# Attention and a gated feed-forward layer on one core: the order of all operations, the steps of the tiles and the turns at the buffers come from lists in place of ranks

## The chip, the core and the metric

The kernel runs on one core of a Trainium2 chip (trn2). The metric is the device time of one execution in microseconds; the median of several runs counts. One more execution was taken with a profiler, and every row of a trace below comes from that one. The engines are named as in the profile: PE multiplies matrices (PEld is its loading of weights, which runs beside it), DVE, ACT and POOL compute on vectors, and SP issues the DMAs.

## What is computed

The reference, cut to what matters:

```python
k_p = k.reshape(B, H, Sp, pool, D).mean(axis=3)      # B 8, H 8, S 576, D 64, pool 8
v_p = v.reshape(B, H, Sp, pool, D).mean(axis=3)
scores = scale * np.matmul(q, k_p.transpose(0, 1, 3, 2))
attn = np.exp(scores - np.max(scores, axis=-1, keepdims=True))
attn = attn / (np.sum(attn, axis=-1, keepdims=True) + 1e-09)
x = np.matmul(attn, v_p)                             # as 4608 tokens x 512
g = x @ w_gate                                       # 512 x 1536
return (g / (1 + np.exp(-g)) * (x @ w_val)) @ w_out  # 1536 x 512
```

All inputs and outputs are float32. The kernel splits operands into a high and a low 16-bit part and adds three products for each, so that the matmuls run on 16-bit numbers.

## The kernel before

The 4608 tokens are nine tiles of 512. Attention goes in 40 pieces of up to 128 queries (`ask` loads the queries of one, `answer` does the rest: scores on PE at L643, the softmax on ACT and DVE, a transposing DMA at L1357 that writes `pt`, the values on PE at L732 to L735 for the first batch and at L742 to L748 for the others, and the high and low parts of x). For the first batch the low part of x is one DVE instruction at L767; for the other batches a second transposing DMA, L1506, brings x into place.

The hidden layer is 12 chunks of 128 rows. `chunk` loads the two input weights of one chunk (L380), decodes them on ACT and DVE, and sums their sizes (L426 on ACT, then a small matmul on PE, L361); `halves_of` then makes the high and low parts. A step is one chunk of one tile. Tiles 0 and 1 take plain steps (`plain_step`, 24 matmuls at L852 to L854 for a gate and 24 for a value, issued by PE in groups of 3). From tile 2 on nearly all are fast steps (`fast_step`, seven block products by Strassen and Winograd at L957, twelve operations: PE, ACT and DVE take turns). In a fast step the ninth operation is PE's product 7, the tenth an ACT copy (L1026), the eleventh a DVE addition (L1027), and the twelfth PE's product 4, which needs both. Each step ends with a tanh on ACT (L799), two DVE instructions (L802, L807) and a store of the hidden values to DRAM (L982). When all nine tiles are done, the output weights are cut (`sums_of_w_out`, `cut`), and the hidden values come back in blocks (`load_block`) for the last products (L1818, L1833, L1834), which go from about 640 us to the end.

The order is the planner's. Each piece of work is a generator, called a line here as in the source; it yields operations with an engine, a cost in ns and the time from which its operands are there, and it asks for buffers. `Order.run` keeps a clock for each engine by these costs, and always emits the operation that could begin first; among those that could begin within a slack, the one with the smallest rank (the tables `RANK` and `KINDS`, and single numbers such as `KEYS`, `SPLITS` or `CHUNKS` for the early part). Buffers go to whoever asks first by rank, `Order.granted`:

```python
            if kind == "get" and self.pools[name]:
                got = min(self.pools[name], key=lambda g: g[0])
```

The instructions of an engine are emitted in that order and each engine runs its own in that order; semaphores hold an instruction until its operands are there. So a late operand holds all that is behind it on the same engine.

Early on PE also gets matmuls of zeros (`warm`, L1273), which nobody reads. The planner puts one on PE, at 300 ns, whenever it holds PE to be free, until the first step has been taken (the loop of up to 120, which ends by the flag `taken`); there are 35.

Which chunk a tile takes next is decided while planning: `first_steps` takes for tiles 0 and 1 what will have landed soonest, and `tile_steps` chooses for a later tile between plain and fast by what is ready `soon`.

Of the kernel before, what the change touches and what calls it, by code (L numbers as in the profile page):

```python
# [23 lines left out]
LAG = 3  # L24
# [59 lines left out]

class Order:
# [7 lines left out]
    def __init__(self, pools):  # L93
# [5 lines left out]
        self.lines, self.flags, self.count = [], {}, 0  # L99
        self.pools = {name: [(0.0, item) for item in items] for name, items in pools.items()}  # L100
# [50 lines left out]
    def start(self, prio, g, sp=None):  # L151
        self.count += 1
        e = {"prio": (*prio, self.count), "g": g}
# [14 lines left out]

    def granted(self):
        for e in sorted(self.lines, key=self.rank(None)):  # L170
# [7 lines left out]
            if kind == "get" and self.pools[name]:  # L178
                got = min(self.pools[name], key=lambda g: g[0])
# [63 lines left out]
def attention_then_swiglu(  # L243
# [227 lines left out]
    def k_load(b, g, at=None):  # L471
# [3 lines left out]
        else:  # L475
            if g == 0:
# [387 lines left out]
    converting, reserved = set(), {}  # L864

    def fast_weights(c):

        if True:
            t = yield flag(("used", FAST_FROM - 1, c))
            t = max(t, (yield flag(("decoded", 9 + c // 3 if c < 9 else c, 1))))  # L870
            yield flag("room")
            home_f, t0 = yield get("fw")
            while c in reserved:
                t = yield flag(("used", reserved.pop(c), c))
            converting.add(c)
# [157 lines left out]
    def tile_steps(i):  # L1033
# [8 lines left out]
        todo = list(range(NCH))  # L1042

        def soon(name):
            found = order.flags.get(name)
            return found is not None and (found if isinstance(found, float) else found[0]) < order.now + 1500

        for at in range(NCH):
            prio = "step", i + 0.01 * at
            plain = [c for c in todo if c not in converting]  # L1050
            fast = [c for c in todo if c in converting]
            ready = [c for c in fast if soon(("w", c))]
            if not plain or ready and soon(("xc", i)):
                txc, xc = yield flag(("xc", i))
                c = (ready or fast)[0]
                tw = yield flag(("w", c))
                order.start(prio, fast_step(i, at, c, x, xc, un, prio, max(t, txc, tw)))
            else:
                c = plain[0] if i < FAST_FROM else plain[-1]
                reserved[c] = i  # L1060
                order.start(prio, plain_step(i, at, c, x, un, prio, t))
            todo.remove(c)
# [9 lines left out]
    def chunk(c):  # L1072
# [12 lines left out]
        tf = yield flag(("decoded", c - 3, 1)) if c > 2 else flag("start")  # L1085
# [27 lines left out]
    def halves_of(c, i, t):  # L1113
# [5 lines left out]
        order.done(("decoded", c, i), t)  # L1119

# [13 lines left out]
    def decoded():  # L1134
        t = 0
        for c in range(NCH):
            t = max(t, (yield flag(("p2w", c))), (yield flag(("decoded", c, 1))))
# [901 lines left out]
```

## Time and profile before

| | us |
|---|---|
| median of 3 runs | 908.55 |
| the 3 runs | 908.24, 908.55, 914.46 |
| the profiled execution | 906.06 |
| its span, first to last instruction | 904.2 |
| PE busy | 879.0 (97%) |
| DVE busy | 736.9 (81%) |
| ACT busy | 615.9 (68%) |

The span is 1.9 us shorter than the profiled execution's own time; that rest lies before the first and after the last instruction that the profile shows. "Busy" counts the time in which at least one instruction of the engine runs, from the profile's spans. Matmuls overlap, and their ends are modelled.

### The profile page before, as it was taken

Reading aid. Unit: us, or ns where it says so; the run is one execution under the profiler, and the core shown is the slowest. Engines: PE = TensorE matmul, PEld = TensorE weight load, DVE = VectorE, ACT = ScalarE, POOL = GpSimd, SP = SyncE. Lnnn points to the kernel's source line nnn. Section 1 sums busy time; section 2 is a strip of 40 time slices with the busy share of each in tenths; the row PEclk is TensorE's granted clock in tenths of the full one; section 3 lists DMA queues with packets and bytes.
Section 4 is the critical chain, followed back from the end, with each engine's and each line's share of the span. In section 5 each row is a group of like instructions: output and inputs, shape, how many; then the busy total and the mean of one; then the engine's idle time right before and its main releaser. Section 6 shows DMA issues by size and latency. Waiting matters only on the chain. (4 is left out here: it accounts for less than half of the span.)

```text
span 904.2 us, 18233 instructions
## 1 busy us (share of the span) xinstructions
PE 879.0 (97%) x6853; PEld 637.2 (70%) x6872; DVE 736.9 (81%) x1175; ACT 615.9 (68%) x1458; POOL 196.6 (22%) x245
## 2 busy tenths in 40 slices
PE   7889999999999999999999999999999999999998
PEld 4475455457788888888888888888885555555554
DVE  6899898899798888879888867568978887686872
ACT  5899855666767755775766755446657778777783
POOL 2465316757811521110011000022100000000000
PEclk9599999999999999999999999999999999999999
DMA  9948997438476498396475543136472624517101
GB/s 352 344 123 230 230 256 177 104 114 220 99 213 154 115 238 171 110 230 182 125 182 139 128 145 129 71 106 238 159 268 71 207 96 163 210 39 273 60 24 71
DMA packets 139129, 148.41 MB, mean 164 GB/s; under 512 B 85792, under 2 KB 107040, under 8 KB 136736
## 3 DMA queue, kind: packets, MB, share of 16 engines
q1 hardware_dynamic: 139040, 147.24, 56.1%
q8 instruction: 54, 0.88, 0.4%
q14 instruction: 35, 0.29, 0.1%
HBM read 87.29 MB, written 40.89 MB: 142 GB/s over the span
## 5 line engine op out<-in xcount | busy, mean ns | idle before, releaser
L957 PEld LDWEIGHTS <-mixed 128*128 128x128 f16 x1494 | 144.1, 98 | 19.9 <-issue 2.3
L957 PEld LDWEIGHTS <-wgv_h 128*128 128x128 f16 x1328 | 128.2, 98 | 20.9 <-issue 4.0
L1833 PE MATMUL ps<-low,wsh 128*128 128x512 bf16 (+1 forms) x408 | 142.2, 357 | 0.4
L957 PE MATMUL ps<-xc,mixed 128*128 128x256 f16 x996 | 130.0, 273 | 0.2
L957 PE MATMUL ps<-xc,wgv_h 128*128 128x256 f16 x664 | 116.5, 272 | 1.6 <-DVE ps L1027 0.9
L799 ACT ACTIVATE hf<-ps,un 128x512 f32<-128x512 f32 (+1 forms) x111 | 75.2, 678 | 62.1 <-PE ps L957 49.6
L957 PE MATMUL ps<-x,wgv_h 128*128 128x256 f16 x664 | 115.9, 273 | 0.0
L802 DVE SCALAR_TENSOR_TENSOR hf<-hf,ps 128x512 f32<-128x512 f32 (+1 forms) x111 | 74.0, 667 | 29.1 <-ACT hf L799 28.6
L807 DVE SCALAR_TENSOR_TENSOR hf<-ps,un,hf 128x512 f32<-128x512 f32 (+1 forms) x111 | 81.1, 730 | 17.8 <-PE ps L957 15.7
L957 PE MATMUL ps<-x,wgv_l 128*128 128x256 f16 x332 | 90.5, 273 | 0.0
L957 PE MATMUL ps<-xc,wgv_l 128*128 128x256 f16 x332 | 90.4, 272 | 0.0
L853 PE MATMUL ps<-x,wgv_h 128*128 128x512 f16 (+1 forms) x224 | 79.7, 356 | 0.5 <-DVE x L767 0.3
L852 PE MATMUL ps<-x,wgv_h 128*128 128x512 f16 (+1 forms) x224 | 79.9, 357 | 0.1
L854 PE MATMUL ps<-x,wgv_l 128*128 128x512 f16 (+1 forms) x224 | 79.8, 356 | 0.0
L1833 PEld LDWEIGHTS <-wsh 128*128 128x128 bf16 x420 | 41.0, 98 | 45.2 <-issue 7.6
L1834 PE MATMUL ps<-top,wsl 128*128 128x512 bf16 x188 | 71.3, 379 | 0.3
L957 PEld LDWEIGHTS <-wgv_l 128*128 128x128 f16 x664 | 64.9, 98 | 7.6
L957 PE MATMUL ps<-x,mixed 128*128 128x256 f16 x498 | 68.0, 273 | 0.7 <-DVE ps L1022 0.3
L1019 ACT COPY ps<-ps 128x256 f32<-128x256 f32 x83 | 30.6, 369 | 49.9 <-PE ps L957 49.5
L662 ACT ACTIVATE sc<-ps,mx 128x72 f32<-128x72 f32 (+1 forms) x208 | 64.0, 330 | 0.6
L1818 PE MATMUL ps<-more,wsh 128*128 128x512 f32 (+1 forms) x216 | 50.9, 383 | 0.0
L1310 DVE TENSOR_REDUCE box<-in 128x144 f32<-128x1152 f32 x36 | 48.0, 1339 | 3.5 <-DMA in<-kv_parts 3.5
(215 smaller groups left out, 1911.0 us busy)
## 6 DMA issues: line engine op xcount, KB each, us to landing
hd<-hf SPq DMA_DIRECT2D x105, 256.0 KB, 2.3
in<-kv_parts SPq DMA_DIRECT2D x42, 576.0 KB, 5.2
ws<-w_all SPq DMA_DIRECT2D x36, 512.0 KB, 5.1
wgv_h<-hd SPq DMA_DIRECT2D x9, 1536.0 KB, 6.7
wgv_l<-hd SPq DMA_DIRECT2D x9, 1536.0 KB, 7.4
out_t<-ob SPq DMA_DIRECT2D x36, 256.0 KB, 3.6
qt<-q_rows SPq DMA_DIRECT2D x32, 256.0 KB, 4.1
wd<-wf SPq DMA_DIRECT2D x12, 256.0 KB, 2.3
```

The lines of the kernel that those rows point to most:

```text
L662: nc.scalar.activation(sc[:n, h], pss[g][:n, j * SP : (j + 1) * SP], AF.Exp, bias=mx[:n, g, j : j + 1], scale=EXPSCALE, accum_out=sm[:n, h ...
L799: nc.scalar.activation(hf, gate, AF.Tanh, scale=un[:, c, 0:1])
L802: nc.vector.scalar_tensor_tensor(out=hf, in0=hf, scalar=1.0, in1=gate, op0=ALU.add, op1=ALU.mult)
L807: nc.vector.scalar_tensor_tensor(out=out, in0=val, scalar=un[:, c, 2:3], in1=hf, op0=ALU.mult, op1=ALU.mult)
L852: nc.tensor.matmul(o, wh, x["h"][:, j, a:e], start=(j == 0), stop=False)
L853: nc.tensor.matmul(o, wh, x["l"][:, j, a:e], start=False, stop=False)
L854: nc.tensor.matmul(o, wl, x["h"][:, j, a:e], start=False, stop=(j == NJ - 1))
L957: nc.tensor.matmul(o, a, b, start=begin and j + n == 0, stop=j == HJ - 1 and n == 2, skip_group_check=True,)
L1310: nc.vector.tensor_reduce(out=dst, in_=part["in"], axis=AX.X, op=ALU.add)
L1818: nc.tensor.matmul(o, next(w_of(k, c, j)), where[0][c // 2][:, c % 2], start=begin and c == 0, stop=False, skip_group_check=True,)
L1833: nc.tensor.matmul(o, top, where[1][:, c], start=False, stop=False, skip_group_check=True)
L1834: nc.tensor.matmul(o, lo, x_up, start=False, stop=c == HC - 1, skip_group_check=True)
```

## The change

`NAMES` gives a name to each line (the generator's name and its numbers, so `answer.3` is piece 3 and `plain_step.0.10.7.0.512` the step number 10 of tile 0, chunk 7). `TURNS` is one list of 3691 such names in the order in which they get a turn to emit an operation; `listed` takes the first of the next 200 whose line has an operation to emit. `HOLDERS` says for each pool who gets which buffer in turn, `JOBS` which step comes when and whether it is fast. `ZEROS` is 35. Nothing is taken by rank as long as the list has a name that can go. Some flags become stricter: `decoded` with 2 means that both halves of a chunk are there, and product 6 of the last stage waits in the plan for the copy of product 1's sum.

The instructions are the same ones: on each engine the same kinds in the same numbers (12210 rows of matmuls and weight loads on PE, 1177 on DVE, 1228 on ACT, 250 on POOL, 389 on SP), and the steps of all tiles come in the same order of chunks. What differs is which operation stands before which. On PE the order is the old one again from the sixth operation of the last products on (651.9 us in the trace), to the end.

```diff
+AHEAD = 200
+ZEROS = 35
+NAMES = (
+    "keys.0.0 keys.0.1 ask.0 values_load.0.0 warm chunk.0 values_load.0.1 chunk.1 first_fields answer.0 values_in.0.0 ask.1 values_load.0.2 "
...
+TURNS = (
+    "0 1 2 3 4 5 4 5 4 6 7 4 4 7 0 4 4 1 4 1 4 4 8 9 10 9 11 12 9 13 5 5 5 13 9 4 5 14 9 7 5 15 9 7 4 16 15 5 17 18 15 19 7 20 21 5 9 15 9 22 15 "
...
+HOLDERS = {
...
+    "qt": (
+        "2/1 11/1 16/1 20/0 32/0 50/1 69/1 78/1 79/0 90/1 121/0 130/1 143/0 144/1 153/0 157/1 174/0 178/1 192/0 209/1 213/0 230/1 231/0 243/0 244/1 "
...
+JOBS = (
+    (0, 0, 0, 0), (0, 1, 0, 0), (0, 2, 0, 0), (0, 0, 256, 0), (0, 1, 256, 0), (0, 2, 256, 0), (0, 3, 0, 0), (0, 4, 0, 0),
...
+    def holds(self, pool, line, item):
+        listed = self.holders.get(pool)
+        return not listed or listed[0] == (line, label(item))
 
     def granted(self):
...
-            if kind == "get" and self.pools[name]:
-                got = min(self.pools[name], key=lambda g: g[0])
+            free = [g for g in self.pools[name] if self.holds(name, e["name"], g[1])] if kind == "get" else ()
+            if free:
+                got = min(free, key=lambda g: g[0])
+                del self.holders.get(name, [])[:1]
...
+    def listed(self):
+        for n, name in enumerate(self.turns[:AHEAD]):
+            for e in self.lines:
+                if e["name"] == name and e["need"][0] == "op":
+                    self.turns.pop(n)
+                    return max(self.free[e["need"][1].rstrip("+")], self.ready(e)), e
+        return None
+
     def run(self):
         while self.lines:
             if self.granted():
                 continue
-            first = None
-            for engine, free in self.free.items():
+            first = self.listed()
+            for engine, free in {} if first else self.free.items():
...
-        for at in range(NCH):
+        for at, (_, c, _, fast) in enumerate([job for job in JOBS if job[0] == i]):
             prio = "step", i + 0.01 * at
-            plain = [c for c in todo if c not in converting]
-            fast = [c for c in todo if c in converting]
-            ready = [c for c in fast if soon(("w", c))]
-            if not plain or ready and soon(("xc", i)):
+            if fast:
                 txc, xc = yield flag(("xc", i))
-                c = (ready or fast)[0]
...
-        while cuts or rest:
...
+        for i, c, a, _ in [job for job in JOBS if job[0] < 2]:
+            names = needs(i, c, a)
+            for name in names:
+                yield flag(name)
...
-        for _ in range(120):
-            if ("taken", 0, WARM) in order.flags:
-                break
+        for _ in range(ZEROS):
...
-                    if k == 7:
-                        t0 = yield flag(("begun", p, 3, j))
+                    t0 = yield flag(("begun", p, k - 4, j))
```

Three places show what moves. The source's lines are numbered anew by the lists: L1273, L643, L732 and L361 of before are L1588, L983, L1072 and L701 after; L767, L1310, L366 and L680 are L1107, L1625, L706 and L1020; L852 to L854 are L1192 to L1194.

The first place is PE ahead of the first values. `spare` with `qt` are the scores of a piece (here of piece 3), `pt` with `spare` the values (here of piece 1), `wm` the sums of a chunk's weights. Before, eleven zero matmuls stand ahead of these scores (the last two are shown), and the values follow at once:

```order
L1273 LDWEIGHTS zeros
L1273 MATMUL ps<-zeros 128x512
L1273 LDWEIGHTS zeros
L1273 MATMUL ps<-zeros 128x512
L643 MATMUL ps<-spare,qt 128x72 x8
L732 LDWEIGHTS spare
L732 MATMUL ps<-pt,spare 128x128
```

After, nine stand ahead (the last is shown):

```order
L1588 LDWEIGHTS zeros
L1588 MATMUL ps<-zeros 128x512
L983 MATMUL ps<-spare,qt 128x72 x8
L1588 LDWEIGHTS zeros
L1588 MATMUL ps<-zeros 128x512
L701 MATMUL ps<-wm,ones 128x2
L1588 LDWEIGHTS zeros
L1588 MATMUL ps<-zeros 128x512
L1588 LDWEIGHTS zeros
L1588 MATMUL ps<-zeros 128x512
L1072 LDWEIGHTS spare
L1072 MATMUL ps<-pt,spare 128x128
```

The scores of piece 3 move two zero matmuls up, three zero matmuls and the small matmul of chunk 2 now stand between them and the values of piece 1.

The second place is DVE ahead of the low part of x for piece 1 (`x<-ps,rr,x`). Before:

```order
L684 RECIPROCAL ri<-sm 128x8
L366 TENSOR_SCALAR p2w<-ps 128x2
L369 RECIPROCAL sw<-p2w 128x2
L366 TENSOR_SCALAR p2w<-ps 128x2
L369 RECIPROCAL sw<-p2w 128x2
L1310 TENSOR_REDUCE spare<-in 128x144
L767 SCALAR_TENSOR_TENSOR x<-ps,rr,x 128x4x128
```

After:

```order
L706 TENSOR_SCALAR p2w<-ps 128x2
L709 RECIPROCAL sw<-p2w 128x2
L1625 TENSOR_REDUCE spare<-in 128x144
L1020 TENSOR_REDUCE sm<-sc 128x8
L1107 SCALAR_TENSOR_TENSOR x<-ps,rr,x 128x4x128
L732 TENSOR_SCALAR ws<-ws 128x1024
L706 TENSOR_SCALAR p2w<-ps 128x2
L709 RECIPROCAL sw<-p2w 128x2
L1625 TENSOR_REDUCE spare<-in 128x144
```

One reduction of keys and values (the one of `kv_part.1.3`), one pair of scales and one shift of a chunk's weights go behind the low part of x; the row sums of piece 3 (L1020) come ahead of it.

The third place is PE in tile 0's step with chunk 7, at the scores of piece 8. Before:

```order
L852 LDWEIGHTS wgv_h
L852 MATMUL ps<-x,wgv_h 128x512
L853 LDWEIGHTS wgv_h
L853 MATMUL ps<-x,wgv_h 128x512
L854 LDWEIGHTS wgv_l
L854 MATMUL ps<-x,wgv_l 128x512
L643 MATMUL ps<-spare,qt 64x72 x8
L852 LDWEIGHTS wgv_h
L852 MATMUL ps<-x,wgv_h 128x512
```

After:

```order
L1192 LDWEIGHTS wgv_h
L1192 MATMUL ps<-x,wgv_h 128x512
L1193 LDWEIGHTS wgv_h
L1193 MATMUL ps<-x,wgv_h 128x512
L1194 LDWEIGHTS wgv_l
L1194 MATMUL ps<-x,wgv_l 128x512
L983 MATMUL ps<-spare,qt 64x72 x8
L1192 LDWEIGHTS wgv_h
```

The rows read alike, since all groups of a plain step do; what moved is that five groups of three matmuls that stood behind these scores (one of chunk 7, four of chunk 8) now stand ahead of them.

## Rows read from the trace of the kernel before

**Rows 1.** The head of the page and the engines' busy time.

```profile
span 904.2 us, 18233 instructions
PE 879.0 (97%) x6853; PEld 637.2 (70%) x6872; DVE 736.9 (81%) x1175; ACT 615.9 (68%) x1458; POOL 196.6 (22%) x245
```

**Rows 2.** Stretch, length; PE, PEld, DVE, ACT, POOL busy (instructions); granted clock, DMA share, GB/s.

```profile
50.00:100.00 50.00, 45.55 (x364) 29.26 (x365) 47.15 (x84) 46.51 (x146) 29.44 (x41) 1.00 0.74 213
100.00:640.00 540.00, 533.23 (x4947) 424.59 (x4948) 453.02 (x812) 347.87 (x1000) 149.43 (x166) 1.00 0.60 159
650.00:900.00 250.00, 248.84 (x1217) 149.47 (x1234) 187.29 (x189) 179.26 (x211) 0.00 (x0) 1.00 0.39 139
```

**Rows 3.** PE's waits, whole run: total us, times, longest us.

```profile
PE ps L742 <- DMA pt<-half: 3.6, 5, 1.6
PE ps L360 <- DVE mx L523: 3.2, 1, 3.2
PE ps L361 <- ACT wgv_h L426: 2.6, 4, 1.1
PE ps L643 <- ACT sc L662: 1.5, 1, 1.5
PE ps L957 <- DVE ps L1027: 0.9, 4, 0.3
PE ps L732 <- DMA pt<-half: 0.5, 1, 0.5
```

**Rows 4.** PE in order of time: start, length, instruction, idle time before it.

```profile
19.57 1.24 PE L1273 MATMUL ps<-zeros 128*128 128x512 f16 x3
24.05 0.59 PE L360 MATMUL ps<-least,ones 128*128 128x1 f32 x2 [3.25 <-DVE mx L523]
26.78 1.99 PE L643 MATMUL ps<-spare,qt 64*128 64x72 f32 x16 [1.26 <-DMA qt<-q_rows]
28.70 7.01 PE L1273 MATMUL ps<-zeros 128*128 128x512 f16 x11
35.64 1.99 PE L643 MATMUL ps<-spare,qt 64*128 64x72 f32 x16
37.56 0.29 PE L732 MATMUL ps<-pt,spare 128*128 128x128 f16 x1
42.57 0.27 PE L732 MATMUL ps<-pt,spare 128*128 128x128 f16 x1
46.25 0.27 PE L853 MATMUL ps<-x,wgv_h 128*128 128x256 f16 x1 [0.31 <-DVE x L767]
99.88 0.71 PE L643 MATMUL ps<-spare,qt 64*64 64x72 f32 x14 [1.46 <-ACT sc L662]
243.36 0.39 PE L742 MATMUL ps<-box,pt 128*128 128x512 f16 x1 [1.63 <-DMA pt<-half]
```

**Rows 5.** SP's queue in order of time.

```profile
1.66 1.33 SPq L627 DMA_DIRECT2D qt<-q_rows  x2
17.82 0.55 SPq L627 DMA_DIRECT2D qt<-q_rows  x1
```

**Rows 6.** DVE and ACT ahead of the first step, in order of time.

```profile
39.49 0.69 ACT L763 ACTIVATE x<-ps,rr 128x512 f16<-128x512 f32 x1 [1.42 <-PE ps L735]
40.52 1.33 DVE L1310 TENSOR_REDUCE spare<-in 128x144 f32<-128x1152 f32 x1
41.77 0.74 DVE L767 SCALAR_TENSOR_TENSOR x<-ps,rr,x 128x512 f16<-128x512 f32 x1
45.50 0.70 DVE L767 SCALAR_TENSOR_TENSOR x<-ps,rr,x 128x512 f16<-128x512 f32 x1
```

**Rows 7.** Granted clock around PE's first long wait, columns as in rows 2.

```profile
20.00:24.00 4.00, 0.75 (x2) 0.10 (x1) 2.95 (x7) 4.00 (x7) 0.25 (x1) 0.99 1.01 394
36.00:40.00 4.00, 4.00 (x36) 3.87 (x35) 3.66 (x8) 2.58 (x7) 1.87 (x3) 0.50 1.03 410
44.00:48.00 4.00, 3.64 (x42) 2.61 (x40) 3.78 (x8) 3.53 (x4) 1.15 (x1) 0.95 0.98 230
```

More of the change, by code (lines that the diff above doesn't have):

```diff
@@ new lines, with named, label @@
+JOBS = (
[14 rows of a table added]
+)
+def named(g):
+    code, given, name = g.gi_code, g.gi_frame.f_locals, [g.gi_code.co_name]
+    for arg in code.co_varnames[: code.co_argcount]:
+        v = given[arg]
+        if isinstance(v, dict):
+            name += [v[key] for key in ("i", "a", "n") if key in v]
+        elif type(v) in (int, str) and arg not in ("t", "t0", "t1", "ts", "tn", "tv"):
+            name.append(v)
+    return ".".join(str(v).replace(" ", "") for v in name)
+def label(item):
+    return str(item[-1] if isinstance(item, tuple) else getattr(item, "__name__", item))
@@ L99, in __init__ @@
         self.lines, self.flags, self.count = [], {}, 0
+        names = NAMES.split()
+        self.turns = [names[int(n)] for n in TURNS.split()]
+        self.holders = {pool: [(names[int(n.split('/')[0])], n.split('/')[1]) for n in given.split()] for pool, given in HOLDERS.items()}
         self.pools = {name: [(0.0, item) for item in items] for name, items in pools.items()}
@@ L152, in start @@
         self.count += 1
-        e = {"prio": (*prio, self.count), "g": g}
+        e = {"prio": (*prio, self.count), "g": g, "name": named(g)}
         e["sp"] = e["prio"] if sp is None else (prio[0], sp, self.count)
@@ L863, in attention_then_swiglu @@
     order.idle = idle
-    converting, reserved = set(), {}
     def fast_weights(c):
         if True:
-            t = yield flag(("used", FAST_FROM - 1, c))
-            t = max(t, (yield flag(("decoded", 9 + c // 3 if c < 9 else c, 1))))
+            t = 0
+            for i in sorted({i for i, n, _, fast in JOBS if n == c and not fast}):
+                t = max(t, (yield flag(("used", i, c))))
+            t = max(t, (yield flag(("decoded", 9 + c // 3 if c < 9 else c, 2))))
             yield flag("room")
             home_f, t0 = yield get("fw")
-            while c in reserved:
-                t = yield flag(("used", reserved.pop(c), c))
-            converting.add(c)
             f = home_f("fw")
@@ L1119, in halves_of @@
         order.done(("decoded", c, i), t)
+        t = max(t, split_at.setdefault(c, t))
+        if (c, "one") in split_at:
+            order.done(("decoded", c, 2), t)
+        split_at[c, "one"] = t
     def factors(c, t):
@@ L1162, in first_steps @@
     def first_steps():
-        cuts = [(c, a) for a in (0, HT) for c in range(LAG)] + [(c, 0) for c in range(LAG, NCH)]
-        rest = list(range(NCH))
         taken = [0, 0]
```

108 lines of the change are left out of this document (79 added, 29 removed), and 222 rows, old and new, of tables (HOLDERS, JOBS, NAMES, TURNS).

## The prediction

> **What bounds the kernel now.** I read the engines' shares first, then the busy time by stretch, then PE's waits, and last the order of time at the places where these waits lie. PE is busy for 879.0 of 904.2 us [rows 1], so all that another order can give back is the 25.2 us in which PE stands still, and time in which it works on what nobody needs. By stretch [rows 2]: from 100 to 640 us, where the steps of the tiles run, PE stands for 540 - 533.2 = 6.8 us; from 50 to 100 us for 4.4 us; from 650 to 900 us for 1.2 us. The other 25.2 - 6.8 - 4.4 - 1.2 = 12.8 us lie ahead of 50 us and behind 900 us. Ahead of 50 us PE isn't the bound: the first real step begins at 46.25 us, when the low part of x is there [rows 4], and PE fills its time with zeros. From 50 to 100 us all three large engines are nearly full (DVE 47.2, ACT 46.5, PE 45.6 of 50 us) [rows 2]: there a wait that goes may come back as another.
>
> **The change, part by part.** No instruction comes or goes, on any engine, and the tiles take their chunks in the old order. So there is no new work to price; the sum is made of waits, against the profiled execution's span of 904.2 us, and the result is taken off the median, 908.55 us (the profiled execution itself took 906.06).
>
> *The way to the first step.* The chain before is: values of piece 1 on PE at 37.56, high part of x on ACT at 39.49, low part on DVE at 41.77, values of piece 0 at 42.57 (there is one bank for them, so they wait for the low part), the low part of piece 0 at 45.50, the first step at 46.25 [rows 4, 6]. Three things move on it. First, before, SP loads the queries of piece 3 third of all, at 1.66 us with those of piece 0, and those of piece 2 only at 17.82, behind much other traffic [rows 5]; they arrive late enough for PE to wait 1.26 us at 26.78 [rows 4]. After, the queries of piece 3 and three of the loads that stood ahead of piece 2's come behind these. The scores of piece 2 should then follow the small matmul at 24.05 nearly at once, 1 to 2 us sooner. Second, between these scores and the values of piece 1 stand 11 zeros and the scores of piece 3 before (7.01 and 1.99 us); after it is 12 zeros and one small matmul more, at 7.01 / 11 = 0.64 us a zero. So the values of piece 1 come 0.3 to 1.3 us sooner; I take 0.7. Third, on DVE the low part of piece 1 loses the reduction ahead of it (1.33 us) and gets the row sums of piece 3 in exchange, which are ready earlier. The high part was done at 39.49 + 0.69 = 40.18, the low part began 1.59 us later; I take 1.3 of that. Together 2.0 us at the first step. Since DVE is full from 50 us on, I count 1.5; bounds 0 (DVE gives nothing on) and 3 us.
>
> *Long waits of PE behind the first step.* Each has its producer and its cover in the two orders, so I compare how far PE's instruction moved with how far its producer moved. The scores of piece 8 waited 1.46 us at 99.88 for an exponential; five groups of three matmuls of plain steps now stand ahead of them, each busy for 0.27 us as the first step's [rows 4]; even with some overlap the 15 are over 3 us of cover: gone. The values that wait for the transposing DMA (L742, five waits, 3.6 us) [rows 3]: three of the five get matmuls ahead or their DMA sooner by more than they waited; the longest, 1.63 us at 243.36 [rows 4], keeps its place on PE, and its DMA passes one load only, so I leave 1.2 us: 2.2 us go. The sums of weights (L361, four waits, 2.6 us): at three of them ACT's sums move up by more than the matmul does; the one of 1.1 us moves up with its producer by the same 1.6 to 1.8 us and stays: 1.3 us go. The values of piece 3 (L732, 0.5 us) get a group ahead and an earlier DMA: gone. That makes 1.46 + 2.2 + 1.3 + 0.5 = 5.5 us.
>
> *Waits inside fast steps.* Product 4 waits for the ACT copy and the DVE addition behind product 7; PE waits there 0.9 us in four waits long enough to be listed [rows 3]. What covers it is the number of other PE operations between products 7 and 4. Of the 83 fast steps, 51 have at most two there before, three of them only one; after, 22 have two and none has fewer. I take 0.8 us off; nothing and 2 us are the bounds, since shorter waits than those listed aren't seen.
>
> *What is late next.* On the other side stands what the lists move too far up. Where a PE operation moved up by more than its producer did, counted with the lengths of what each passed, it would be late; I find seven such places of over half a microsecond, 5.6 us together, all in the fast and plain steps, mostly an ACT copy behind the PE product just ahead. Each is what it would be if all else stayed, and PE's operations behind it can't pass it. Bounds: nothing, when the producers gain with PE, and 6.8 us, as much as PE stands still in these 540 us now [rows 2]. The trace shows that 83 fast steps with one or two operations of cover cost little (0.9 us listed), so I stay nearer to the lower end: 2.0 us.
>
> *The last stage.* Behind 651.9 us PE's order is the old one and it stands still for 1.2 of 250 us. ACT and DVE move there, a few stores by ten and more microseconds, but stores of finished output hold nobody while a buffer is free. I put it at 0, bounds -0.5 and +2.
>
> Sum: -1.5 - 5.5 - 0.8 + 2.0 = -5.8 us: a span of 898.4, a median of 902.7 us.
>
> One rule bears on the zeros. PE's granted clock is at the full level (2.4 GHz) until 24 us and at half (1.2 GHz, 0.50) after the wait of 3.25 us [rows 4, 7]; a zero takes 1.24 / 3 = 0.41 us at the first level, 0.64 at the second. The Trainium skill ("TensorE: Matmul & The Clock Gate", section "Part 1: The HAM clock gate") says that an idle array is throttled and that activity takes the throttle away. In this trace it falls after the wait, as the page says, but from 36 to 40 us, after 8 us of zeros without a pause, the clock is still 0.50. By the page's rule the values would run at the full level in the new order, and the first step would come a further 2 us or so sooner; by the row they stay at half. I follow the row.
>
> **The rivals.** (a) *The waits only change places.* For: DVE and ACT are full from 50 to 100 us, so a PE that comes sooner to a chunk waits for its halves there; and the 5.6 us of operations moved too far up would about eat the 5.5 us of waits covered. Against: the moved operands were looked at one by one, and most producers moved with their users. Then -1.5 to +1.5: 908.5 us. (b) *Far more goes.* If all of the 4.4 us before 100 us and 6 of the 6.8 us behind go, nothing new comes, and the first step is 2 us sooner, it is -12.4, about 896 us. For: none of the long waits was left wholly uncovered except two; against: the waits of 1.63 and 1.1 us keep their places, and DVE is too full for all of the 4.4. (c) *The half clock falls on the steps.* Now the half level lies over zeros, scores and values, and ends just before the first step: from 44 to 48 us the mean is 0.95 again [rows 7], 20 us behind the wait. The zeros are spread otherwise in the new order: should PE stand still between 27 and 34 us, because the queries come sooner and the nine zeros are used up before the scores of piece 3 have their operands, a fall of the clock there, as after the wait of 3.25 us, would carry a stretch of 20 us into the steps. Then some 20 us at half speed, with 10 us of step work in them, cost 10 us more: 902.7 + 10 = 912.7, and 918 if the first two terms don't come either. It decides at a wait of about the length of the one at 24.05 us, behind 27 us. Against: nine zeros at 0.64 us last till 32 us or so, and the operands of these scores are there by then. That the lists aren't followed can be put aside: the rows of the three places have moved.
>
> **How the numbers follow.** The forecast gets 0.50 (898 to 906), (a) 0.22 (906 to 911), (b) 0.19 (893 to 898), (c) 0.09 (911 to 919). Leaving out a tenth at each end gives 896 to 911. One per cent, 9 us, is about what a measurement of this kernel can tell from no change. Faster by more than that means under 899.5: all of (b) and a tenth of the forecast, 0.19 + 0.05 = 0.24. Slower by more than that, over 917.6: half of (c) and a trifle for a hold-up at a buffer that I didn't see, 0.06. The rest, 0.70, lies within one per cent.
>
> **What would show it right or wrong.** Right: the first step's matmuls at 44 to 45 us in place of 46.25; no wait of over 1 us at the scores of piece 8; the values behind L742 waiting under 2 us in total, with the longest near 243 us; PE standing still for about 4 us from 100 to 640 us; PE's time from the first of the last products to the end unchanged within a microsecond. Wrong: a first step later than 46.25 us or a half clock behind it, which would be (c); waits of PE for ACT's copies in the fast steps of 3 us and more together, which would be (a); or PE's idle time from 100 to 640 us under 2 us, which would be (b).

## The result

The changed kernel takes 900.15 us, the median of 4 runs (897.28 to 901.47), against 910.01 for the kernel before in the same runs (908.24 to 914.46): a ratio of 0.988, 95% interval 0.9835 to 0.9926. It is faster, by 1.2% within 0.7 to 1.7%. In three later sets of runs the kernel before had medians of 907.47, 906.68 and 907.67 us (27, 23 and 23 runs), so its 910.01 is a little high, and against those 900.15 is 6.5 to 7.5 us less. Forecast were 5.8 us less and a median of 902.7.

The page of the profiled execution (900.0 us, with a span of 898.2), for [rows 1]:

```profile
span 898.2 us, 18137 instructions
PE 876.0 (98%) x6872; PEld 637.5 (71%) x6872; DVE 732.5 (82%) x1175; ACT 613.5 (68%) x1458; POOL 193.7 (22%) x245
```

PE is busy for 3.0 us less and stands still for 22.2 us in place of 25.2. Even of these last 3.0 us, 1.0 is no wait: the trace of before has 6853 of PE's 6872 matmuls [rows 1], and the 19 that it lacks, all behind 678 us, leave gaps of some 55 ns each. The trace after lacks none. So only 2.0 of the 6.0 us are less standing still. Part of PE's "busy" time is time at half clock and gaps too short to be taken for idle, and both got less.

Busy time by stretch, columns as in [rows 2]:

```profile
50.00:100.00 50.00, 47.60 (x375) 30.36 (x374) 47.11 (x84) 47.18 (x145) 27.81 (x37) 1.00 0.76 213
100.00:640.00 540.00, 533.52 (x4990) 428.46 (x4989) 451.37 (x818) 347.86 (x1003) 145.55 (x169) 1.00 0.58 159
```

From 50 to 100 us PE stands for 2.4 us in place of 4.4; from 100 to 640 us for 6.5 in place of 6.8, though the waits of [rows 3] are mostly gone. PE's waits now, the whole list:

```profile
PE ps L1588 <- POOL zeros L1585: 2.1, 1, 2.1
PE ps L1193 <- DVE x L1107: 2.0, 1, 2.0
PE ps L700 <- DVE mx L863: 1.7, 1, 1.7
PE ps L701 <- ACT wgv_h L766: 1.7, 2, 1.3
PE ps L1082 <- DMA pt<-half: 1.6, 3, 0.7
PE ps L1295 <- ACT rs L1355: 1.3, 3, 0.6
PE ps L1295 <- DVE ps L1360: 1.1, 3, 0.4
PE ps L1295 <- DVE ps L1365: 1.0, 2, 0.5
PE ps L983 <- DMA qt<-q_rows: 1.0, 1, 1.0
PE ps L983 <- DVE sc L1092: 0.9, 1, 0.9
PE ps L1192 <- ACT x L1103: 0.8, 1, 0.8
PE ps L1295 <- ACT ps L1357: 0.6, 1, 0.6
PE ps L1295 <- DVE hf L1147: 0.4, 1, 0.4
PE ps L1072 <- DVE x L1107: 0.2, 1, 0.2
```

(L1082 is L742 of before, L701 is L361, L700 is L360, L983 is L643, L1295 is L957.) The values behind the transposing DMA fell from 3.6 to 1.6 us, the sums of weights from 2.6 to 1.7, the scores of piece 8 from 1.5 to nothing. New are the waits of fast steps for ACT's copies (1.3 and 0.6), more for DVE's additions, and 2.0 and 0.8 us at the first step. What went and what came are about equal. From the first step on, the list of before has 10.2 us (9.1 in [rows 3] without L360, and four rows of 0.2 or 0.3 us), and the list above has 11.4 (all but L1588, L700, L1072 and the wait for the queries, `q_rows`, which lie ahead of that step). So what was gained behind the first step lies in gaps that this list leaves out.

PE on the way to the first step, for [rows 4], and ACT and DVE there, for [rows 6]:

```profile
23.49 0.38 PE L700 MATMUL ps<-least,ones 128*128 128x1 f32 x2 [1.72 <-DVE mx L863]
24.27 1.36 PE L983 MATMUL ps<-spare,qt 64*128 64x72 f32 x16
25.56 5.73 PE L1588 MATMUL ps<-zeros 128*128 128x512 f16 x9
35.29 0.31 PE L1072 MATMUL ps<-pt,spare 128*128 128x128 f16 x1
39.52 0.22 PE L1072 MATMUL ps<-pt,spare 128*128 128x128 f16 x1 [0.23 <-DVE x L1107]
43.00 0.27 PE L1192 MATMUL ps<-x,wgv_h 128*128 128x256 f16 x1 [0.79 <-ACT x L1103]
45.26 0.27 PE L1193 MATMUL ps<-x,wgv_h 128*128 128x256 f16 x1 [1.98 <-DVE x L1107]
```

```profile
37.78 0.67 ACT L1103 ACTIVATE x<-ps,rr 128x512 f16<-128x512 f32 x1
...
41.04 1.33 ACT L784 ACTIVATE wgv_h<-mixed,sw 128x512 f16<-128x512 f32 x2
42.28 0.67 ACT L1103 ACTIVATE x<-ps,rr 128x512 f16<-128x512 f32 x1
...
38.73 0.74 DVE L1107 SCALAR_TENSOR_TENSOR x<-ps,rr,x 128x512 f16<-128x512 f32 x1
...
42.29 2.25 DVE L789 SCALAR_TENSOR_TENSOR wgv_l<-mixed,sw,wgv_h 128x512 f16<-128x512 f32 x2
44.46 0.74 DVE L1107 SCALAR_TENSOR_TENSOR x<-ps,rr,x 128x512 f16<-128x512 f32 x1
```

The chain comes 3 us sooner down to the values of piece 0 (39.52 in place of 42.57), and then loses two of them: on ACT the high part stands behind two halves of weights, on DVE the low part behind two of 2.25 us together, and the first step's L1193 begins only 1.0 us sooner than before (45.26 against 46.25). The granted clock there, for [rows 7]:

```profile
20.00:24.00 4.00, 2.17 (x15) 1.22 (x13) 3.67 (x10) 4.00 (x10) 0.37 (x1) 1.00 0.95 336
36.00:40.00 4.00, 3.66 (x27) 2.39 (x25) 3.93 (x8) 3.94 (x13) 3.39 (x3) 0.67 0.91 289
44.00:48.00 4.00, 2.75 (x14) 2.00 (x14) 4.00 (x7) 3.04 (x7) 2.91 (x3) 0.68 1.07 317
```

Cut finer, it is 0.50 from 25.0 to 38.6 us, behind the wait of 1.72 us, and again from 45.4 to 48.9, behind the waits of 0.79 and 1.98; before it was 0.50 once, from 23.9 to 44.4. So it is 17 us at half in place of 20.5, but 3.5 of them now lie on the first step.

For the rest I count what PE loses from start to start: for each operation of PE (a product of a fast step, a group of a plain step, a piece's scores) the time from its start to that of the next, less the lower quartile of that time for its kind in the kernels before and after. Gaps of any size and half clock are in it. The sums stand by work done since the first step, so that a column is the same amount of work whatever the order:

```
us lost, by us of PE's work behind the first step's start
kernel            first step    0-40  40-110  110-180  180-300  300-500  500-575    all
before                45.7       5.3     4.9      2.1      6.2      3.5      1.6   69.3
after                 43.0       6.9     2.0      3.4      2.8      1.8      3.7   63.4
r1_ramp_new           42.9       9.5     4.5      2.2      7.1      3.4      1.6   71.1
r2_ramp_old           46.0       4.6     2.0      3.7      2.6      1.0      3.7   63.6
r3_fast_new           45.8       5.2     5.3      4.5      3.5      1.2      3.7   68.9
r4_zeros_old          45.6       4.4     7.3      4.3      5.0      4.6      1.6   72.7
r5_waits_early        46.0       5.1     5.2      1.9      7.7      3.5      1.6   70.9
r6_waits_fast         46.0       5.2     5.4      4.2      7.0      3.4      1.6   72.8
r7_x_sooner           41.7       7.3     2.0      4.5      2.2      1.3      3.7   62.6
r8_after_waits        42.6       6.1     2.3      4.9      3.3      1.1      3.7   63.9
r9_last_tile_old      42.1       7.2     2.0      4.1      2.4      1.8      1.7   61.3
r10_tiles_4_to_7      46.1       5.2     5.5      6.1      6.0      0.9      1.7   71.4
r11_fast_old          43.1       7.0     2.1      6.5      5.0      3.7      1.6   68.9
r12_product4_sooner   42.3       6.8     2.0      4.6      6.1      5.7      5.9   73.4
```

The first fast step begins at 151 us of work, tile 4 at 277, tile 8 at 519. 69.3 - 63.4 = 5.9 us is, but for rounding, the whole difference of the spans (6.0). It is made of -2.7 + 1.6 = -1.1 until 40 us of work, -2.9 in the rest of tile 0 and the start of tile 1, +1.3, -3.4 in tiles 2 to 4, -1.7 up to tile 7, and +2.1 in tile 8, where the new order is the worse one (each rounded by itself). Each row is one profiled execution, and the column from 110 to 180 differs by 2 us and more between executions of the old order there (the last section), so the +1.3 in it shows nothing. The stage behind 651.9 us took 248.04 us before and takes 248.07.

### The profile page after: what moved, and what is told of

It reads as the page before. It is cut to its first block, busy times and chain, and to the rows that moved or that the text cites. A ratio compares the mean times of both kernels' runs of the same rounds, so it can differ in the third digit from the quotient of the medians.

```text
span 898.2 us, 18137 instructions
## 1 busy us (share of the span) xinstructions
PE 876.0 (98%) x6872; PEld 637.5 (71%) x6872; DVE 732.5 (82%) x1175; ACT 613.5 (68%) x1458; POOL 193.7 (22%) x245
## 5 line engine op out<-in xcount | busy, mean ns | idle before, releaser
L1295 PEld LDWEIGHTS <-mixed 128*128 128x128 f16 x1494 | 144.5, 98 | 20.3 <-issue 2.4
L2148 PE MATMUL ps<-low,wsh 128*128 128x512 bf16 (+1 forms) x420 | 146.7, 358 | 0.0
L1295 PEld LDWEIGHTS <-wgv_h 128*128 128x128 f16 x1328 | 127.8, 98 | 21.0 <-issue 4.4
L1295 PE MATMUL ps<-xc,mixed 128*128 128x256 f16 x996 | 130.7, 273 | 0.6 <-ACT ps L1357 0.6
L1295 PE MATMUL ps<-xc,wgv_h 128*128 128x256 f16 x664 | 116.6, 273 | 1.6 <-DVE ps L1365 1.0
L1295 PE MATMUL ps<-x,wgv_h 128*128 128x256 f16 x664 | 116.7, 273 | 1.3 <-ACT rs L1355 1.3
L1295 PE MATMUL ps<-x,wgv_l 128*128 128x256 f16 x332 | 90.5, 273 | 0.0
L1295 PE MATMUL ps<-xc,wgv_l 128*128 128x256 f16 x332 | 90.5, 272 | 0.0
L1147 DVE SCALAR_TENSOR_TENSOR hf<-ps,un,hf 128x512 f32<-128x512 f32 (+1 forms) x111 | 80.7, 729 | 10.7 <-PE ps L1295 8.1
L1193 PE MATMUL ps<-x,wgv_h 128*128 128x512 f16 (+1 forms) x224 | 80.5, 359 | 2.0 <-DVE x L1107 2.0
L1192 PE MATMUL ps<-x,wgv_h 128*128 128x512 f16 (+1 forms) x224 | 80.6, 360 | 0.9 <-ACT x L1103 0.8
L1194 PE MATMUL ps<-x,wgv_l 128*128 128x512 f16 (+1 forms) x224 | 80.5, 359 | 0.0
L1295 PEld LDWEIGHTS <-wgv_l 128*128 128x128 f16 x664 | 64.9, 98 | 7.6
L1295 PE MATMUL ps<-x,mixed 128*128 128x256 f16 x498 | 68.0, 273 | 1.1 <-DVE ps L1360 1.1
L1365 DVE TENSOR_TENSOR ps<-ps,rs 128x256 f32<-128x256 f32 x83 | 35.3, 427 | 32.9 <-ACT ps L1364 32.7
L1355 ACT COPY rs<-ps 128x256 f32<-128x256 f32 x83 | 31.0, 373 | 33.2 <-PE ps L1295 22.8
```

Source lines behind the costliest of these rows:

```text
L1147: nc.vector.scalar_tensor_tensor(out=out, in0=val, scalar=un[:, c, 2:3], in1=hf, op0=ALU.mult, op1=ALU.mult)
L1192: nc.tensor.matmul(o, wh, x["h"][:, j, a:e], start=(j == 0), stop=False)
L1193: nc.tensor.matmul(o, wh, x["l"][:, j, a:e], start=False, stop=False)
L1194: nc.tensor.matmul(o, wl, x["h"][:, j, a:e], start=False, stop=(j == NJ - 1))
L1295: nc.tensor.matmul(o, a, b, start=begin and j + n == 0, stop=j == HJ - 1 and n == 2, skip_group_check=True,)
L1365: tp = yield op("DVE", 430, lambda: nc.vector.tensor_add(s, s, rs), tp)
```

## The experiments

All kernels are the changed source with other numbers in `TURNS` and `HOLDERS`; with the order of the kernel before as lists, the instructions come as in before (in the traces of r4 and r6 DVE, ACT, POOL and SP have exactly its order), so the lists themselves change nothing. In the diffs a row is an entry of `TURNS` as PE carries it out: the line's name and the number of its operation (in a fast step 1 is product 5, 3 product 1, 5 and 6 are products 6 and 2, 8 is product 3, 9 product 7, 12 product 4). A plain step has eight groups of three matmuls on PE, 12 matmuls for the gate and 12 for the value, not 24 for each as said ahead of the prediction.

### Which part of the order: r1, r2, r3, r11

One kernel's list up to a point, then the other's without what already stands. r1 against before (and so on up to the first step's first entry):

```diff
 answer.0#1
+values_in.0.0#1
 warm#11
+values_in.0.1#1
+answer.1#1
 warm#12
...
```

> The new order up to the first matmul of the first step, the old order from there on. Theory A (the gain has two sources of about equal size, the way to the first step and the small gaps inside the fast steps): the first step's first matmul near 43.0 us as after the change, against 45.7 before; from there to the last stage 606 us as before; in all 2 to 3 us less than before, a span of 901 to 902. Rival B (the whole gain is made ahead of the first step and in the first tile, the rest of the order is worth nothing): 5 us or more less, a span under 899.5. Rival C (what comes sooner to the first step waits there again): 0 to 1 us less.

r2 against before, from the first step's first entry on:

```diff
 plain_step.0.0.0.0.256#5
+plain_step.0.0.0.0.256#6
 answer.2#12
-plain_step.0.0.0.0.256#6
 plain_step.0.0.0.0.256#7
+chunk.3#9
...
```

> The old order up to the first matmul of the first step, the new order from there on. Theory A: the first step at 45.7 us as before, from there to the last stage 603 us or a little less, since no half clock falls on the first step; 3 to 4 us less than before, a span of 900 to 901. Rival B: 0 to 1 us less.

r3 against before, from the first fast step on:

```diff
 fast_step.2.1.0#1
+fast_step.2.2.1#1
+fast_step.2.1.0#3
+fast_step.2.1.0#5
 plain_step.2.0.11.0.512#6
-fast_step.2.2.1#1
...
```

> The old order up to the first fast step, the new order from there on. Theory A: the first fast step at about 208 us as before, the stretch from there to the last stage 3 us shorter than the 443.6 us of before: 2.4 us less in waits and gaps of under 0.2 us, and PE's waits for the copies and additions of the fast steps, listed with 0.9 us and 0.3 us before, no larger than the 3 to 4 us after the change; a span near 901. Rival B: within 1 us of before.

r11 against after, from the first fast step on:

```diff
 plain_step.2.0.11.0.512#3
+plain_step.2.0.11.0.512#4
+plain_step.2.0.11.0.512#5
 fast_step.2.1.0#1
-plain_step.2.0.11.0.512#4
...
```

> The new order up to the first fast step, the old order from there on; with the runs so far this makes the fourth of two times two. Theory O (the parts add): 3 us less than before, as 900.14 - 903.34 and 900.15 - 903.34 say, near 904. Rival P (the gain ahead of the fast steps stands only when the fast steps are in the new order too, since the hand-over is fitted): 0 to 1 us less.

```
new order in                     median us   before   ratio (95%)
r1   the way to the first step     907.38    907.47   1.0000 (0.9982 to 1.0017)
r2   all but that way              900.14    907.47   0.9920 (0.9897 to 0.9944)
r3   the fast steps alone          903.34    907.47   0.9952 (0.9934 to 0.9970)
r11  all ahead of the fast steps   904.16    907.67   0.9956 (0.9940 to 0.9973)
```

The parts add. The fast steps give 4.1 us (r3), what lies ahead of them 3.5 (r11) or 907.47 - 4.13 - 900.14 = 3.2 (r2 against r3), and all of this between the first step and the first fast step, for the new way to the first step gives 0.0 (r1). The 4.1 us of the fast steps have tile 8's loss in them (r9, below). Theory A was wrong on the way to the first step: it gave r1 2 to 3 us and r2 only 3 to 4, and r2 measured 7.3. The first step of r1 did come at 42.92 us, and Rival C held. What r1 won is gone at once, in a wait of PE:

```profile
42.92 0.27 PE L1194 MATMUL ps<-x,wgv_h 128*128 128x256 f16 x1 [0.79 <-ACT x L1105]
45.18 0.37 PE L1195 MATMUL ps<-x,wgv_h 128*128 128x256 f16 x1 [1.99 <-DVE x L1109]
...
56.63 0.23 PE L1074 MATMUL ps<-pt,spare 128*128 128x128 f16 x1 [2.33 <-DMA pt<-half]
```

The values of piece 3 waited 0.5 us in [rows 3]. With half clock on the first step and once more in the windows from 56 to 60 and 60 to 64 us (means of 0.76 and 0.82) r1 loses 9.5 us in the first column against 5.3.

### Does the clock or a wait hold the way to the first step: r4, r7

r4 is the kernel before with zeros in PE's two waits:

```diff
 warm#24
+pooled_values.0#2
 warm#25
...
 warm#28
+answer.2#1
 warm#29
```

> The kernel before with ten more zero matmuls on PE, seven in its wait of 3.25 us at 24 us and three in the wait of 1.26 us at 26.8 us; all else in the old order. If PE's long wait is what brings the half clock: the granted clock stays at 1.00 until the first step. Theory D (the half clock holds the way to the first step, by zeros and scores that take longer): the first step 2 us or more sooner than 45.7, and the span 2 to 4 us shorter. Rival E (DVE and the operands hold it): the first step within 1 us of 45.7 though the clock is full, and the time within 1 us of before. Should the clock still fall at 24 us, the wait wasn't its cause.

It took 908.44 us against 907.47, ratio 1.001 (0.9994 to 1.0025), and the first step began at 45.65 us. The clock by its windows, and PE's waits:

```profile
24.00:28.00 4.00, 3.62 (x28) 1.88 (x27) 3.87 (x10) 3.85 (x7) 1.54 (x1) 1.00 1.23 220
28.00:32.00 4.00, 3.50 (x10) 0.86 (x9) 3.71 (x7) 3.90 (x13) 0.58 (x1) 1.00 1.03 409
32.00:36.00 4.00, 1.83 (x23) 1.59 (x23) 2.86 (x4) 4.00 (x21) 2.14 (x3) 0.91 1.19 303
36.00:40.00 4.00, 3.83 (x21) 2.38 (x20) 3.86 (x12) 3.29 (x8) 1.87 (x3) 0.50 1.02 405
```

```profile
35.48 0.26 PE L1074 MATMUL ps<-pt,spare 128*128 128x128 f16 x1 [2.17 <-DMA pt<-half]
...
41.73 0.27 PE L1074 MATMUL ps<-pt,spare 128*128 128x128 f16 x1 [1.27 <-DVE x L1109]
```

With the waits filled the clock stays at 1.00 where it was 0.50, so the waits brought it down. But PE then comes sooner to the values of piece 1, waits 2.17 us there for their DMA, the clock falls after all, and the first step stays where it was: Rival E. Cut finer, it is 0.50 from 35.3 to 45.6 us: 10.2 us in place of 20.5. So the half clock ahead of 35.3 us cost nothing; the rest of it r4 doesn't take away, and so doesn't price.

r7 is the changed kernel with both parts of x of piece 0 ahead of the halves of weights that held them. On DVE:

```diff
 answer.3#7
+answer.0#14
 halves_of.1.1#2
 halves_of.2.0#2
-answer.0#14
```

> The changed kernel with both parts of x of piece 0 ahead of the halves of weights of the first steps: on ACT the high part stands two places sooner, on DVE the low part two places sooner. The first step's first matmul of the other side of x starts near 43 us in place of 45.26, without the wait of 1.98 us, and the granted clock should not fall behind it (it was 0.50 from 45.4 to 48.9 us). If the first 50 us bound the kernel: 2 to 3.5 us less than after the change. If what DVE and ACT still owe in tile 0 bounds it, as the new way to the first step gave 0.0 by itself: within 0.7 us of the changed kernel's 900.15.

900.33 us against 906.68, ratio 0.9930 (0.9908 to 0.9952): no different from the changed kernel. The first step's L1194 came at 42.69 us with a wait of 0.73 us, and the next wait was there:

```profile
42.69 0.27 PE L1194 MATMUL ps<-x,wgv_h 128*128 128x256 f16 x1 [0.73 <-DVE x L1108]
46.76 0.22 PE L1073 MATMUL ps<-pt,spare 128*128 128x128 f16 x1 [2.06 <-DMA pt<-half]
```

It also brought the half clock onto the steps again (0.72 in the mean from 45 to 50 us). A sooner first step isn't what bounds this kernel, in either order. What does bound tile 0 stays open.

### Long waits, by PE's order alone: r5, r6, r8

r5 is the kernel before with five waiting instructions of PE set back, two of them here:

```diff
 plain_step.0.9.6.0.512#7
-chunk.9#8
 plain_step.0.9.6.0.512#8
 plain_step.0.10.7.0.512#1
+chunk.9#8
 plain_step.0.10.7.0.512#2
 plain_step.0.10.7.0.512#3
-answer.8#1
 plain_step.0.10.7.0.512#4
...
 plain_step.0.11.8.0.512#1
+answer.8#1
```

> The kernel before, in which five instructions of PE that waited longest behind the first step and ahead of the fast steps stand one to four of PE's operations later: the sums of weights of chunks 3 and 9 (1.09 and 0.76 us of wait), the scores of piece 8 (1.46), the values of piece 11 (0.48), the scores of piece 15 (0.31); all the rest in the old order. Theory F (what a long wait costs goes when other work of PE stands ahead of it): 3 to 4 us less than before, as much as the stretch between the first step and the first fast step gave in the runs so far (903.34 - 900.14 = 3.2). Rival G (these waits only change places, because DVE and ACT are full there): 0 to 1 us less. Rival H (the new order of DVE and ACT in this stretch is what gives): also 0 to 1 us less, with the five waits gone and others in their place.

r6, likewise in tiles 2 and 3:

```diff
 fast_step.2.6.5#6
-answer.18#11
 fast_step.2.5.4#12
...
 fast_step.2.6.5#9
+answer.18#11
 fast_step.2.7.6#3
```

> The kernel before, in which three instructions of PE in tiles 2 and 3 that waited for a transposing DMA stand one to four of PE's operations later: the values of pieces 18, 19 and 25 (1.63, 0.98 and 0.30 us of wait); all the rest in the old order. Theory F: 2.5 to 3 us less, most of the 4.1 us that the new order of the fast steps gave alone (907.47 - 903.34). Rival I (the small gaps inside the fast steps give the 4.1 us: product 4 with one or two operations of cover loses 3.8 us in the kernel before, counted from start to start, against 1.5 after): 0 to 1.5 us less.

r8, the changed kernel with seven of its own set back, one of them:

```diff
 plain_step.1.11.11.0.512#2
-answer.15#1
 plain_step.1.10.10.0.512#3
 plain_step.1.10.10.0.512#4
+answer.15#1
```

> The changed kernel with the seven instructions of PE that wait longest behind the first step one to three operations later: the sums of weights of chunks 4 and 9 (0.41 and 1.31 us), the values of pieces 6, 18 and 19 (0.45, 0.69, 0.42), the scores of piece 15 (0.91), product 4 of step 6 of tile 5 (0.49). Theory F: 3 to 4 us less than the changed kernel, near 896.5. Rival G: within 1 us of 900.15.

r5 took 906.60 us against 906.68, ratio 0.9999 (0.9986 to 1.0012); r6 909.37, ratio 1.0025 (1.0008 to 1.0042), a little slower; r8 899.86, ratio 0.9919 (0.9902 to 0.9937), as the changed kernel. Theory F fell three times. The waits themselves went, and others came: in r5 at the sums of chunk 10, in r6 at the scores of piece 19, in r8 at a fast step that waits for ACT's copy.

```profile
101.86 0.38 PE L703 MATMUL ps<-wm,ones 128*128 128x2 f32 x2 [1.92 <-ACT wgv_h L768]
```

```profile
249.21 1.11 PE L985 MATMUL ps<-box,qt 64*128 64x72 f32 x14 [0.90 <-ACT sc L1102]
```

```profile
223.27 0.38 PE L1296 MATMUL ps<-x,wgv_h 128*128 128x256 f16 x2 [1.86 <-ACT rs L1356]
```

ACT and DVE kept their order (but for two instructions of DVE in r5) and so their lateness, and PE meets it at the next of their results. In r5 PE is at the sums of chunk 10 at 99.9 us in place of 102.5, but ACT has them only 0.6 us sooner (first before, then r5):

```profile
102.25 0.20 ACT L426 ACTIVATION_READ_ACCUMULATOR wgv_h<-mixed,least 128x1 f32 x1
102.50 0.38 PE L361 MATMUL ps<-wm,ones 128*128 128x2 f32 x2
```

```profile
101.61 0.20 ACT L768 ACTIVATION_READ_ACCUMULATOR wgv_h<-mixed,least 128x1 f32 x1
```

In the new order the same stretches lose 2.9 and 3.4 us less. Setting back the waiting instructions of PE doesn't give that; that it comes from the orders of ACT and DVE moving along with PE's is the likely reason, but it is inferred and not shown. No run has PE's whole new order with ACT's and DVE's old one, so which producer counts most stays open.

### Small gaps, and the last tile: r10, r12, r9

r10 is the kernel before with the new order in tiles 4 to 7 alone:

```diff
 fast_step.4.0.0#9
+fast_step.4.2.2#1
 fast_step.4.1.1#3
-fast_step.4.2.2#1
 fast_step.4.0.0#12
...
```

> The old order but for tiles 4 to 7, which have the new one. In these tiles no wait of PE is over 0.5 us in either order, so only small gaps differ. Theory M (small gaps): by the profiles so far these tiles lose 2.7 us in the old order (0.8 + 1.0 + 0.5 or 0.3 + 0.8 or 0.9 + 0.4, less what lies ahead of tile 4) against 0.8 in the new one, so 1.5 to 2 us less than before. Rival N (only waits of half a microsecond and more, all of them ahead of tile 4, make the 4.1 us of the fast steps): 0 to 0.5 us less.

905.02 us against 907.67, ratio 0.9969 (0.9954 to 0.9984): 2.6 us less, where neither order has a listed wait of PE of half a microsecond. That is Theory M, and more than its 1.5 to 2 us; in the table the column from 300 to 500 falls from 3.5 to 0.9. Its other columns are those of the old order, 110 to 180 with a clock fall besides.

r12 is the changed kernel with product 4 of 36 fast steps set forward, the orders of the other engines as they were:

```diff
 fast_step.2.2.1#6
+fast_step.2.1.0#12
 fast_step.2.3.2#1
 answer.16#11
-fast_step.2.1.0#12
```

> The changed kernel in which product 4 of 36 fast steps stands sooner on PE, so that two of PE's operations lie between products 7 and 4 in place of three to six; 59 of 83 steps then have two, and 51 of the kernel before had two or one. Theory Q (cover of product 4 is what the small gaps are made of): each loses some 60 ns at two operations, as the 48 of the kernel before did in the mean, 2 us in all, with half a microsecond more from products whose cover falls beside it: 1.5 to 3 us more than the changed kernel. Rival R (two are enough where ACT and DVE come in time, as 22 such steps of the changed kernel lost 7 ns each): 0 to 0.7 us more.

910.17 us, ratio to before 1.0035 (1.0020 to 1.0050), so 10 us more than the changed kernel. The theory that came nearest (Q) gave 1.5 to 3, less than a third of it. What PE waits for is the addition behind product 7:

```profile
PE ps L1296 <- DVE ps L1366: 8.3, 13, 1.6
```

In the changed kernel the same row has 1.0 us in two waits. By the number of PE's operations between products 7 and 4, steps and mean loss at product 4:

```
                       1           2            3
before             3, 295 ns   48,  60 ns   31, -11 ns
after                  -       22,   7 ns   25,  53 ns
r12_product4_sooner    -       59, 177 ns    9,  88 ns
```

The cover by itself doesn't say the loss. Two operations cost 7 ns where the list gave DVE and ACT the time, and 177 ns where PE alone was moved (22 of the 59 are the old ones, so about 280 for the moved).

r9 is the changed kernel with the old order from the first step of tile 8 on:

```diff
 fast_step.8.1.1#5
+fast_step.8.0.0#12
 fast_step.8.1.1#6
 fast_step.8.2.2#3
-fast_step.8.0.0#12
...
```

> The new order up to tile 8, the old order from the first step of tile 8 on. In the five profiles with the new order the last tile's steps lose 3.7 us from start to start of PE's operations against 1.7 in those with the old one. Theory K (the loss belongs to the order of this tile alone): 1.5 to 2 us less than the changed kernel, near 898.3, and PE's waits behind 590 us under 0.5 us. Rival L (it is the price of what was gained before, and comes back elsewhere): within 0.7 us of the changed kernel's 900.15.

897.10 us against 907.67, ratio 0.9878 (0.9859 to 0.9898), the fastest of all. It is 3.0 us below the changed kernel's 900.15. The two did not run side by side, but r2, r7 and r8, which have the new tile 8 too, stand at 0.992 to 0.993 of before, some 4 us above r9 by the ratios. The stretch from 585 to 640 us, after the change, in r9, and before:

```profile
585.00:640.00 55.00, 52.50 (x473) 45.94 (x471) 43.40 (x68) 31.80 (x70) 17.12 (x12) 1.00 0.40 140
```

```profile
585.00:640.00 55.00, 54.57 (x492) 48.01 (x490) 45.15 (x77) 33.24 (x72) 16.45 (x12) 1.00 0.48 163
```

```profile
585.00:640.00 55.00, 54.73 (x496) 48.18 (x495) 41.40 (x69) 31.85 (x70) 16.45 (x12) 1.00 0.50 173
```

PE stands for 0.4 us in place of 2.5. Theory K: the new order gives at least 2 us away there. The trace accounts for these 2; why the times say 3 to 4 isn't known. Five waits of the changed kernel lie in this stretch, the largest two for ACT's copies:

```profile
633.77 0.38 PE L1295 MATMUL ps<-x,wgv_h 128*128 128x256 f16 x2 [0.62 <-ACT rs L1355]
635.83 0.81 PE L1295 MATMUL ps<-xc,mixed 128*128 128x256 f16 x6 [0.59 <-ACT ps L1357]
```

In r9 there is one, of 0.15 us.

## Why the prediction was right, step by step

The time came within 3 us of the forecast and inside its 898 to 906. That is in part luck: by the columns of the table gains and losses are -10.7 and +5.0 us (1.3 of these by chance), where the terms have -7.8 and +2.0, and what the terms miss cancels. By the ratio of 0.988 the gain is a little more than the one per cent inside which the prediction saw 0.70; against the later medians of before it is 0.7 to 0.8%.

- *The way to the first step, -1.5.* Until 40 us of work the profile has -1.1, but by itself this way is worth 0.0 (r1), and without it the rest gains as much (r2). The step that failed is "I count 1.5": its lower bound of 0 was the case. The chain did come 3.0 us sooner as far as the values of piece 0, more than the 2.0 worked out: the scores of piece 2 began 2.5 us sooner (24.27 in place of 26.78), not 1 to 2, and the values of piece 1 2.3 us (35.29 in place of 37.56), not 0.7. The 1.3 us on DVE are there: the low part begins 0.3 us behind the high part's end (38.73 and 38.45), before 1.6. What I left out is what the new order puts ahead of the last link, 2.25 us on DVE and 1.33 on ACT, so that L1193 starts at 45.26 us and not at 44 to 45. But r7, which takes that away, is no faster either: a sooner first step is no time here.
- *Long waits, -5.5.* As forecast the scores of piece 8 wait for nothing, the values behind L742 lost 2.0 of 3.6 us (2.2 forecast), the sums of weights 0.9 of 2.6 (1.3 forecast), piece 3 all of its 0.5. That makes 4.9 us that went, and from 40 to 300 us of work the loss fell by 2.9 - 1.3 + 3.4 = 5.0. But the argument was the cover on PE, and r5 and r6 show that this alone gives nothing at eight such places: 906.60 and 909.37. The step that was too short is "I compare how far PE's instruction moved with how far its producer moved": the next user of the same late engine has to be followed as well.
- *Inside fast steps, -0.8.* Right way, too small. From 300 to 500 us of work it is -1.7, and r10 alone gives 2.6 in time (its interval means 1.5 to 4.2). I took the 0.9 us of waits long enough to be listed; start to start, product 4 lost 48 x 60 + 3 x 295 ns = 3.8 us before.
- *What is late next, +2.0.* Too small, and hardly the seven places. New in the list of waits are 2.5 us at the first step (2.0 and 0.8, where it was 0.3), 3.0 in the fast steps (4.4 in place of 1.4) and 0.6 at the scores of piece 15 (0.9 in place of 0.3): 6.1 us. In the table that is +1.6 up to 40 us of work and +2.1 in tile 8, which r9 confirms. The scores of piece 15 are late as worked out in kind; the long new waits of fast steps are others, most of them in tiles 2 and 8. The step that failed is "so I stay nearer to the lower end".
- *The last stage, 0.* 248.04 and 248.07 us.
- *The frame.* That only PE's standing still could be given back was wrong. Short gaps and half clock in PE's busy time were worth more, 4 of the 6 us, and [rows 2] can't show them; "PE standing still for about 4 us from 100 to 640 us" failed (6.5), because PE now stands for 2.5 us from 585 to 640 us, in tile 8, where it stood for 0.3. And of the 1.2 us behind 650 us, 1.0 are matmuls that the trace lacks.
- *Rivals.* (c) came in small: the clock did fall onto the first step, behind waits of 0.79 and 1.98 us, for 3.5 us in place of 20; 15 matmuls from 45.47 us on took 3.2 us, where 0.11 each at full clock would make 1.6. It isn't what decides, for r2, whose first step has the full clock, takes the same time. (Its 918 us don't add up: 912.7 with the first two terms, 7.0 us, given back is 919.7.) (a), that waits only change places, is what the list of waits shows from the first step on (10.2 and 11.4 us). In time it is so where only PE's order moved (r5, r8) and for the way to the first step (r1), not for the whole change. (b) had the path wrong, for new waits did come. r9 with 897.10 us lies about a microsecond from its 896, but with waits in it that (b) held to be gone.

The rule of the Trainium skill ("TensorE: Matmul & The Clock Gate", section "Part 1: The HAM clock gate") that an idle array is throttled has its counterpart in r4: no wait, no fall. That activity takes the throttle away fits the return at 48.9 us, behind steps from 45.26 us on, and not the 20.5 us before. In the changed kernel the clock was back at 38.6 us, so the values of piece 1 ran at half, as by the row, and those of piece 0 at full, as by the rule. It decides nothing: the 2 us between the two lie at the first step, and a first step that came sooner (r1, r7) took no time off.

## What to carry to other kernels

Moving a waiting instruction back on its own engine bought nothing here, three times, for the engine that it waited for was as late for the next one; look for the next user of that engine before counting the wait as gone. The change moved producers and users, and gained in the same stretches. Where an engine is 97% busy, count its losses from start to start by kind of operation: gaps of 60 ns, 48 times, were worth more than the listed waits of 0.9 us. An order can be tried by stretches: take the better half of each of two orders at a point where both have done the same work, as r9 did for about 3 us.

## What the runs showed of the hardware that I had not expected

The low level of PE's clock has no one length: 20.5 us before, 10.2 in r4, 13.6 and 3.5 us in the changed kernel, though PE was busy for 3.7 us and more of each 4 us from 28 to 44 us, over most of the longest one.

The same order has two outcomes at one place. The scores of piece 15 wait 0.31 us in the kernel before, and 1.64 us in r3, which has the old order as far as that:

```profile
197.36 1.37 PE L985 MATMUL ps<-box,qt 64*128 64x72 f32 x14 [1.64 <-ACT sc L1102]
```

There the clock falls for a few microseconds (0.76 and 0.82 in the two windows from 196 to 204 us), and before it didn't (1.00 in both, PE busy for all of the 8 us):

```profile
196.00:200.00 4.00, 2.64 (x18) 1.68 (x19) 4.00 (x9) 3.56 (x12) 3.35 (x4) 0.76 0.53 131
200.00:204.00 4.00, 4.00 (x17) 1.68 (x16) 3.58 (x2) 3.37 (x18) 2.76 (x5) 0.82 0.77 203
```

So one profile of the old order can be 2 us and more better than the next (110 to 180 us of work: 2.1 before, 4.2 to 4.5 in r3, r4 and r6). Its times spread over 904 to 911 us. Why the wait is long in some executions wasn't found out.
